# Another chunking of the score rows, and two block products that change places in the MoEs' up stages

## The chip, the cores and the metric

One core of a Trainium2 chip. The metric is the device time of one execution in microseconds, the median over runs.

## The reference

Attention with mixing over the heads, then two feed-forward stages ("MoEs" without routing), all in float32:

```python
scores = scale * np.matmul(q, k.transpose(0, 1, 3, 2))        # 4 x 12 x 448 x 448, head_dim 64
scores = np.einsum('bhij,hg->bgij', scores, w_pre)
scores = scores - np.max(scores, axis=-1, keepdims=True)
attn = np.exp(scores)
attn = attn / (np.sum(attn, axis=-1, keepdims=True) + 1e-09)
attn = np.einsum('bhij,hg->bgij', attn, w_post)
x = np.matmul(attn, v)                                        # then 1792 tokens x 768
...
h = x @ w_in                                                  # 768 -> 2048
y = (h * np.clip(h + 3.0, 0.0, 6.0) / 6.0) @ w_out            # 2048 -> 768
...
out = (((y @ w1) * (y @ w2)) @ w3) @ w_out2                   # 768 -> 1024 -> 1024 -> 768
```

## The kernel before, in words

**A planner writes the order.** Each piece of work is handed to `Plan.add` with its engine (or a choice of engines), a cost, a due time and its dependencies. `Plan.run` then plays the engines forward, takes on each the ready piece that is due first, and so writes out five fixed lists, one per queue: PE (TensorE), ACT (ScalarE), DVE (VectorE), POOL (GpSimd) and SP (the DMAs). On the chip every engine works its own list strictly in order and waits on semaphores. The table `URGE` (line 79) holds some 90 numbers that shift the due times; with other numbers all five lists come out differently, though the work is the same.

**Attention.** The query rows of a batch are cut into groups of ten rows; `GROUPS` (line 34) says how many groups each of four chunks has. `scores` (line 497) multiplies one chunk with the keys of two heads at a time, and ACT or DVE copies the result (sc) to the tile s. `mix` (line 531) works on a **slot** of two groups: SP gathers the rows of all heads of a group from s into g; PE mixes the heads (pre); DVE takes the row maximum; ACT the exponential, with its sum; DVE makes the weights wt from the sum; PE mixes and transposes again (post), and ACT or DVE copies that to pth or ptl. `values` (line 622) multiplies with v when half a batch (a unit) is done: three groups of four heads, each in two halves. Its result (val) is copied to one of two buffers x and stored to xdram by SP. Scores, pre, post, val and the later products share four PSUM buffers of two banks.

**MoEs.** A float32 product is three products of rounded parts (high x high, high x low, low x high). Two batches at a time go through a scheme of seven block products for eight, `seven` (line 892): with two PSUM tiles, `pair` (36 matmuls, 9 to a product) and `other` (27), it issues p1, p5, p6, p2, p3, p7 and p4. p1, p6, p7 and p4 go to the same bank of `pair`, p7 and p4 on top of what is there. ACT copies p1, p5 and p6 away (line 911: k1, k5, k6), since the next products add to those banks; DVE adds p2, p3 and p7 to the copies (line 914: c11 and c12 into t, c22 into v). p7 waits for k6, and p4 waits for c22. With `final` set, as the last output stage alone had it, p7 and c22 come before p3 and c12:

```python
k6 = keep(3, t, 1, cs, (p6,))
p2 = times(3, 4, as_, True, after=(p5,))
c11 = plus(4, t, 0, as_, (p2, k1))
p7 = times(5, 5 if final else 6, cs, False, after=(k6,))
c22 = plus(5 if final else 6, v, 0, cs, (p7, k5))
p3 = times(4, 6 if final else 5, bs, False, after=(k5, p7) if final else (k5,))
c12 = plus(6 if final else 5, t, 1, bs, (p3, k6))
p4 = times(6, 9, cs, False, after=(c22,))
```

`up_pair` (line 1007) is the first MoE's up stage for batches 1 and 2 (eight runs of `seven`; batches 0 and 3 go through a plain product beside it). `step` (line 1307) is the second MoE's up stage (sixteen runs); each next run's p1 may start after p7. Weights come as 64-bit floats and are turned to 32 bits by ACT and DVE (lines 790 to 802) all through the first MoE. Near the end of `step`, ACT and DVE also split and combine the inputs of the output stage (tiles orig, gh, act of 1792 elements).

Of the kernel before, what the change touches and what calls it, by code (L numbers as in the profile page):

```python
# [25 lines left out]
KC = DM // 128  # L26
# [4 lines left out]
ROWS = 12 * SET  # L31
GROUP = 2 * SET
BEFORE = 64 - ROWS
GROUPS = [12, 12, 11, 10]
G0 = [sum(GROUPS[:c]) for c in range(5)]
BLOCKS = (G0[4] + 1) // 2
LEN = [GROUP * g for g in GROUPS[:3]]
# [38 lines left out]
    return np.concatenate([order[u, :UNITS[u]] for u in range(2)])  # L76


URGE = dict(pPool=164.025, pACT=19693.834, pDVE=67507.971, pOut=433.371, pGuard=127.43, pCopy=293.188, pRest=69.604, pEvac=133.63, load0=-532.161, load=1034.863, gather=-351.175, pre=-489.029, max=-802.835, exp=-111.088, norm=-1250.143, post=102.75, evac=54.755, values=484.451, step=60.485, vload=1145.281, vload0=-1112.753, lead=-45.053, begin=89.262, consts=-98.616, moe=992.206, rows=1666.907, win=-476.319, wout=252.873, w34=-78.816, w2=109.341, unit0=29.551, unit1=70.923, down1=1322.478, unit2=1085.737, down2=538.008, wo=-207.504, wd=12.243, narrow=887.826, sums=1153.357, w34us=361.925, pHalf=138.291, halve=522.107, gsum=1604.135, joined=-2053.191, pairs=-159.136, lag=-1931.661, mix=-30.819, wo1=1020.065, stay=81.809, apart=2024.643, hHost=-16.855, hSP=788.66, hPE=152.667, hACT=95.962, hDVE=66.109, hPool=210.181, gatherA=-479.669, preA=428.762, maxA=391.052, expA=-367.699, normA=131.345, postA=215.656, evacA=537.477, gatherZ=1037.083, preZ=660.309, maxZ=151.309, expZ=3.296, normZ=1160.431, postZ=410.099, evacZ=-506.584, valuesA=-143.638, valuesZ=61.436, rowsZ=35.402, winZ=172.502, upZ=-145.507)


GS = ("g0", "g1", "g2", "g3")
# [184 lines left out]
def attention_moe(ctx: ExitStack, tc, qd, kd, vd, consts, w_in, w_out, w1, w2, w3t, w4, out):  # L267
# [409 lines left out]
    for ci in range(16):  # L677
        s0 = cstart[ci - 1] * U0 + URGE["begin"] if ci else -120
        s1 = cstart[ci] * U0 + URGE["lead"] if ci else -35
        for hp in range(H // 2):  # L680
            prio = s0 + hp * (s1 - s0) / 6
# [210 lines left out]
    def seven(prio, K, ws, xs, before, after=(), final=False):  # L892

        pair, other = Buf("up"), Buf("up")
        t, v = Buf("t"), Buf("v")
        cs, bs, as_ = (View(pair, lambda t: t[:, 0, :S]), View(other, lambda t: t[:, 0, :S]), View(other, lambda t: t[:, 1, :S]))

        def times(n, at, o, start, new=(), after=()):
            (bufs, parts), (xh, xl) = ws[n], xs[n]

            def emit():
                take(*new)
                for c in range(K):
                    wh, wl = (part()[:, col(c)] for part in parts)
                    mm(o(), wh, xh.t[:, c], start and c == 0, False, skip_group_check=not start)
                    mm(o(), wh, xl.t[:, c], False, False, skip_group_check=not start)
                    mm(o(), wl, xh.t[:, c], False, c == K - 1, skip_group_check=not start)
            return plan.add("PE", 600 * K, prio(at), emit, read=(*bufs, xh, xl), new=new, hold=(o.of,), after=after)

        def keep(at, x, k, o, after):  # L910
            return plan.add("ACT", 530, prio(at), lambda: nc.scalar.copy(x.t[:, k], o()), after=after, hold=(o.of, x))  # L911

        def plus(at, x, k, o, after):
            return plan.add("DVE", 620, prio(at), lambda: nc.vector.tensor_tensor(out=x.t[:, k], in0=o(), in1=x.t[:, k], op=ALU.add), after=after, hold=(o.of, x))  # L914

        p1 = times(0, 0, cs, True, (pair, t, v), (*before, *after))
        k1 = keep(0, t, 0, cs, (p1,))
        p5 = times(1, 1, bs, True, (other,), (p1,))
        k5 = keep(1, v, 0, bs, (p5,))
        p6 = times(2, 3, cs, False, after=(k1,))  # L920
# [8 lines that stand above are left out]
        return t, v, cs, p7, p4, (p2, p3), c11, c12, c22, keep  # L929
# [12 lines left out]
    rows, w_ins, w_outs, lasts = {}, {}, {}, {}  # L942
# [64 lines left out]
    def up_pair(fg, before):  # L1007

        at = M1 + F * fg + 2 * U1 + URGE["lag"]
        prio = lambda n: at + n * 2 * U1 / 7  # L1010
        t, v, cs, p7, p4, (p2, p3), c11, c12, c22, _ = seven(prio, KC // 2, joined1[fg], made1, before)
        r = Buf("rl")

        def relu(k, x, port, after):
            def emit():
                if k == 0:
                    take(r)
                nc.scalar.activation(out=r.t[:, k], in_=x(), func=ACTF.Relu, bias=3.0)
            return plan.add("ACT", 535, prio(6.5 + k * 2.5), emit, after=after, new=() if k else (r,), hold=(r, x.of), port=port)

        def gated(k, x, o, after, port):
            return plan.add("DVE", 620, prio(6.5 + k * 2.5), lambda: nc.vector.scalar_tensor_tensor(out=o(), in0=r.t[:, k], scalar=6.0, in1=x(), op0=ALU.min, op1=ALU.mult), after=after, hold=(r, x.of, o.of), port=port)

        def half(x, k):
            return View(x, lambda t: t[:, k])
        r2 = Buf("rl")

        def relu2():
            take(r2)
            nc.scalar.activation(out=r2.t, in_=t.t, func=ACTF.Relu, bias=3.0)  # L1030

        def gated2():
            nc.vector.scalar_tensor_tensor(out=t.t, in0=r2.t, scalar=6.0, in1=t.t, op0=ALU.min, op1=ALU.mult)
        a2 = plan.add("ACT", 918, prio(6), relu2, after=(c11, c12), new=(r2,), hold=(t,), port=True)
        g2 = plan.add("DVE", 1084, prio(6), gated2, after=(a2,), hold=(t, r2), port=True)
        a0 = relu(0, half(v, 0), True, (c22,))
        g0 = gated(0, half(v, 0), half(v, 0), (a0,), True)
        a1 = relu(1, cs, False, (p4, a0))
        g1 = gated(1, cs, half(v, 1), (a1,), False)
        b0, b1 = ORDER[2:]  # L1040
        gates[fg, b0] = gates[fg, b1] = [
            plan.add("SP", 1300, prio(7), lambda: nc.sync.dma_start(out=g1dram[fg, :, 1:3, 0], in_=t.t), after=(g2,), hold=(t,)),
            plan.add("SP", 700, prio(9), lambda: nc.sync.dma_start(out=g1dram[fg, :, b1, 1], in_=v.t[:, 0]), after=(g0,), hold=(v,)),
            plan.add("SP", 700, prio(9), lambda: nc.sync.dma_start(out=g1dram[fg, :, b0, 1], in_=v.t[:, 1]), after=(g1,), hold=(v,))]
        return (p7,), (p2, p3, p4)
# [248 lines left out]
    def blocks(prio, i):  # L1294

        same = lambda t: t
        wa, jb, wd, ja = (fetch(prio, "raw", (x, same), x.shape[-1], (after,)) for x, after in (
            (w2dram[i], kept["w2", i]), (jbdram[i], joined[i, 1]), (w1dram[i, :, 384:], kept["w1", i]), (jadram[i], joined[i, 0])))
        made = []
        for x, h in ((wa, 0), (jb, 0), (jb, 1), (wa, 1), (ja, 1), (ja, 0), (wd, 0)):  # L1300
            o = Buf("block")
            made.append(split(prio, 384, x, lambda x=x, h=h: f(x.t)[:, h * 384:(h + 1) * 384], (o,), lambda o=o: o.t[:, 0], lambda o=o: o.t[:, 1]))
        return made
# [3 lines left out]
    def step(pr, i, before, xs):  # L1307

        at = M2 + U2 * (8 * pr + i)
        prio = lambda n: at + n * U2 / 7  # L1310
        t, v, cs, p7, p4, p3, c11, c12, c22, _ = seven(prio, KC // 2, blocks(at + URGE["w2"], i), xs, before)

        def gate2(at, x, k, o, y, after, port):
            def emit():
                nc.vector.scalar_tensor_tensor(out=x.t[:, k], in0=o(), scalar=1.0 / 36.0, in1=y(), op0=ALU.mult, op1=ALU.mult)
            return plan.add("DVE", 620, prio(at), emit, after=after, hold=(o.of, y.of, x), port=port)

        g1 = gate2(9, t, 0, cs, View(t, lambda t: t[:, 0]), (p4, c11), False)
        g2 = gate2(6.5, t, 1, View(t, lambda t: t[:, 1]), View(v, lambda t: t[:, 0]), (c12, c22), True)
        pair_ = ORDER[2 * pr:2 * pr + 2]  # L1320
        for k, b in enumerate(pair_):
            gates2[i, b] = plan.add("SP", 700, prio(10), lambda k=k, b=b: nc.sync.dma_start(out=g2dram[i // 2, :, b, i % 2], in_=t.t[:, k]), after=((g1, g2)[k],), hold=(t,))
        return (p7,), p4
# [119 lines left out]
```

## Time and profile before

| what | before |
|---|---|
| median of 3 runs | 1187.79 us (1187.32 to 1189.89) |
| the profiled execution: time | 1183.64 us |
| the profiled execution: span, first to last instruction | 1181.8 us |
| mean granted TensorE clock | 0.994 of full |
| PE (TensorE) busy | 1148.5 us, 97% |
| DVE (VectorE) busy | 775.4 us, 66% |
| ACT (ScalarE) busy | 656.8 us, 56% |
| POOL (GpSimd) busy | 130.3 us, 11% |

The stages on PE: attention to about 361 us, the first MoE's up stage to 572, its down stage to 802, a product of two weight matrices to 869, the second MoE's up stage to 1077, the output to the end. Matmuls are pipelined and their ends are modelled, so that rows of one engine can overlap by some tenths of a microsecond; the idle time in brackets is the engine's own. "A <- B" after a wait names what ended it.

### The profile page before, as it was taken

Reading aid. Unit: us, or ns where it says so; the run is one execution under the profiler, and the core shown is the slowest. Engines: PE = TensorE matmul, PEld = TensorE weight load, DVE = VectorE, ACT = ScalarE, POOL = GpSimd, SP = SyncE. Lnnn points to the kernel's source line nnn. Section 1 sums busy time; section 2 is a strip of 40 time slices with the busy share of each in tenths; the row PEclk is TensorE's granted clock in tenths of the full one; section 3 lists DMA queues with packets and bytes.
Section 4 is the critical chain, followed back from the end, with each engine's and each line's share of the span. In section 5 each row is a group of like instructions: output and inputs, shape, how many; then the busy total and the mean of one; then the engine's idle time right before and its main releaser. Section 6 shows DMA issues by size and latency. Waiting matters only on the chain.

```text
span 1181.8 us, 28260 instructions
## 1 busy us (share of the span) xinstructions
PE 1148.5 (97%) x11376; PEld 978.2 (83%) x11376; DVE 775.4 (66%) x1290; ACT 656.8 (56%) x1262; POOL 130.3 (11%) x335
## 2 busy tenths in 40 slices
PE   8899989999899999999999999999999999999998
PEld 3476656666568999999999999998899998998998
DVE  3766555666478888848755557656754578479682
ACT  7778687787576666527545444434343344335452
POOL 1163343622111000001000000000000000000000
PEclk9999989999999999999999999999999999999999
DMA  6746655846665576747988889987965437478641
GB/s 221 221 148 232 173 191 175 250 169 195 200 205 181 166 255 205 244 152 240 330 286 316 263 312 342 323 291 244 315 218 158 130 129 277 143 234 276 211 153 70
DMA packets 132939, 261.36 MB, mean 221 GB/s; under 512 B 11880, under 2 KB 75208, under 8 KB 132808
## 3 DMA queue, kind: packets, MB, share of 16 engines
q1 hardware_dynamic: 132808, 259.55, 66.2%
q8 instruction: 89, 1.46, 0.5%
q14 instruction: 42, 0.34, 0.1%
HBM read 153.54 MB, written 67.26 MB: 187 GB/s over the span
## 4 chain that ended last, share of the span: by engine, by line
PE 88%; DMA 5%; DVE 3%; ACT 1%; issue 1%; SPq 1%; POOL 0%; DVEq 0%; ACTq 0%; POOLq 0%
PE up L275 41%; PE dn L275 19%; PE pre L275 6%; PE post L275 6%; PE sc L275 6%; PE w L275 5%; PE val L275 5%; DMA xdram<-x 1%; DMA stg<-xdram 1%; DMA raw<-w2dram 1%; DMA g<-s 1%; DMA both<-xdram 1%; DMA first<-w_in 1%; DVE act L278 0%; DVE t L914 0%
## 5 line engine op out<-in xcount | busy, mean ns | idle before, releaser
L275 PE MATMUL up<-act,block 128*128 128x448 f32 x1008 | 203.9, 364 | 4.8 <-DVE v L914 4.8
L275 PEld LDWEIGHTS up<-act,block 128*128 128x128 f32 x1008 | 190.2, 189 | 18.2 <-DVE v L914 5.5
L275 PE MATMUL dn<-gs,act 128*128 128x448 f32 x720 | 147.9, 362 | 0.0
L275 PEld LDWEIGHTS dn<-gs,act 128*128 128x128 f32 x720 | 135.1, 188 | 8.9
L275 PEld LDWEIGHTS post<-wt,e 60*64 60x64 f32 x5040 | 97.1, 135 | 52.9 <-issue 20.1
L275 PE MATMUL up<-act,wide 128*128 128x448 f32 x660 | 139.6, 364 | 0.6 <-DVE v L914 0.3
L275 PEld LDWEIGHTS up<-act,wide 128*128 128x128 f32 x660 | 123.1, 188 | 11.6 <-DVE v L914 1.1
L567 DVE TENSOR_REDUCE m<-pre 128x2 f32<-128x896 f32 (+1 forms) x92 | 99.8, 1088 | 44.5 <-PE pre L275 43.7
L573 ACT ACTIVATE e<-pre,m 128x448 f32<-128x448 f32 (+1 forms) x184 | 117.0, 641 | 11.0 <-DVE m L567 7.4
L412 ACT CAST block<-raw 128x384 fp32r<-128x384 f32 x107 | 54.6, 514 | 109.2 <-PE up L275 86.2
L275 PE MATMUL post<-wt,e 60*64 60x60 f32 x5040 | 100.7, 222 | 12.2 <-issue 6.9
L275 PE MATMUL pre<-g,wih 64*64 64x448 f32 x720 | 96.2, 568 | 6.2 <-ACT x L412 4.3
L790 ACT ACTIVATE raw<-raw 128x384 f32<-128x384 f32 (+1 forms) x140 | 70.6, 522 | 38.2 <-DMA raw<-w 23.9
L275 PE MATMUL up<-act,wb 128*128 128x448 f32 x432 | 87.6, 363 | 0.0
L275 PEld LDWEIGHTS up<-act,wb 128*128 128x128 f32 x432 | 81.0, 188 | 5.6 <-ACT t L911 0.3
L278 DVE TENSOR_TENSOR block<-raw,block 128x384 fp32r<-128x384 f32 x112 | 60.9, 554 | 34.8 <-ACT block L412 34.5
L914 DVE TENSOR_TENSOR t<-up,t 128x448 f32<-128x448 f32 x60 | 37.2, 621 | 66.2 <-PE up L275 61.2
L798 ACT ACTIVATE raw<-raw 128x768 f32<-128x768 f32 (+1 forms) x70 | 55.5, 795 | 41.8 <-DVE raw L796 41.7
L412 ACT COPY s<-sc 120x896 f32<-120x896 f32 (+2 forms) x77 | 68.3, 911 | 10.1 <-PE sc L275 9.6
L802 DVE SCALAR_TENSOR_TENSOR raw<-raw 128x384 int32<-128x384 int32 (+1 forms) x140 | 70.6, 538 | 1.4
L275 PE MATMUL dn<-gs,wo 128*128 128x448 f32 x336 | 71.1, 362 | 0.0
L275 PE MATMUL w<-wm,w 128*128 128x512 f32 (+1 forms) x384 | 66.6, 335 | 0.1
(137 smaller groups left out, 1713.7 us busy)
## 6 DMA issues: line engine op xcount, KB each, us to landing
g<-s SPq DMA_DIRECT2D x180, 210.0 KB
raw<-w SPq DMA_DIRECT2D x48, 384.0 KB
graw<-g1dram SPq DMA_DIRECT2D x32, 448.0 KB
raw<-w_out SPq DMA_DIRECT2D x32, 384.0 KB
raw<-w_in SPq DMA_DIRECT2D x28, 384.0 KB
g1dram<-t SPq DMA_DIRECT2D x24, 448.0 KB
raw<-w3t SPq DMA_DIRECT2D x32, 256.0 KB
vv<-vd SPq DMA_DIRECT2D x12, 640.0 KB
```

What stands on the lines that cost most here:

```text
L275: nc.tensor.matmul(o, lhsT=lt, rhs=rh, start=start, stop=stop, **kw)
L278: eng.tensor_tensor(out=o, in0=a, in1=b, op=ALU.subtract)
L412: nc.scalar.copy(o, i)
L567: nc.vector.tensor_reduce(out=m.t[used], in_=pre.t[used, :, :S], axis=AX.X, op=ALU.max, negate=True)
L573: nc.scalar.activation(out=e.t[used, a_], in_=pre.t[used, a_, :S], func=ACTF.Exp, bias=m.t[used, a_:a_ + 1], accum_out=z.t[used, a_:a_ + 1])
L790: nc.scalar.mul(value()[:, halves[i]], f(bits(i))[:, :, 1], 2.0 ** -112)
L798: nc.scalar.activation(out=f(y), in_=f(y), func=ACTF.Prelu, alpha=-2.0 ** 32)
L802: two(out=m.t[:, halves[i]], in0=bits(i)[:, :, 0], scalar=29, in1=m.t[:, halves[i]], op0=ALU.logical_shift_right, op1=ALU.bitwise_or)
L914: return plan.add("DVE", 620, prio(at), lambda: nc.vector.tensor_tensor(out=x.t[:, k], in0=o(), in1=x.t[:, k], op=ALU.add), after=after, h ...
```

## The change

The last two chunks of score rows get 12 and 9 groups for 11 and 10, `up_pair` and `step` call `seven` with `final=True`, and every number of `URGE` is another.

```diff
-GROUPS = [12, 12, 11, 10]
+GROUPS = [12, 12, 12, 9]
...
-URGE = dict(pPool=164.025, pACT=19693.834, pDVE=67507.971, pOut=433.371, pGuard=127.43, pCopy=293.188,
+URGE = dict(pPool=267.274, pACT=19707.749, pDVE=67519.092, pOut=411.463, pGuard=243.897, pCopy=232.932,
...
-        t, v, cs, p7, p4, (p2, p3), c11, c12, c22, _ = seven(prio, KC // 2, joined1[fg], made1, before)
+        t, v, cs, p7, p4, (p2, p3), c11, c12, c22, _ = seven(prio, KC // 2, joined1[fg], made1, before, final=True)
...
-        t, v, cs, p7, p4, p3, c11, c12, c22, _ = seven(prio, KC // 2, blocks(at + URGE["w2"], i), xs, before)
+        t, v, cs, p7, p4, p3, c11, c12, c22, _ = seven(prio, KC // 2, blocks(at + URGE["w2"], i), xs, before, final=True)
```

**The tenth of the sixteen runs in the second MoE, on PE.** up_11877 is this run's `pair`, up_11900 its `other`, up_11763 the `pair` of the run before and up_12017 that of the next. Before: p1, p5, the last run's p4, p6, p2, p3, p7, p4, and the next run's p1:

```order
L275 MATMUL up_11877<-act3_6285,block_11747 128x448 x9
L275 MATMUL up_11900<-act0_5554,block_11761 128x448 x9
L275 MATMUL up_11763<-act_6453,block_11723 128x448 x9
L275 MATMUL up_11877<-act0_5554,block_11775 128x448 x9
L275 MATMUL up_11900<-act_6453,block_11789 128x448 x9
L275 MATMUL up_11900<-act_6453,block_11802 128x448 x9
L275 MATMUL up_11877<-act_6453,block_11817 128x448 x9
L275 MATMUL up_11877<-act_6453,block_11835 128x448 x9
L275 MATMUL up_12017<-act3_6285,block_11846 128x448 x9
```

Now (`pair` up_11881, `other` up_11897):

```order
L275 MATMUL up_11881<-act3_6285,block_11750 128x448 x9
L275 MATMUL up_11897<-act0_5555,block_11765 128x448 x9
L275 MATMUL up_11769<-act_6453,block_11729 128x448 x9
L275 MATMUL up_11881<-act0_5555,block_11781 128x448 x9
L275 MATMUL up_11897<-act_6453,block_11799 128x448 x9
L275 MATMUL up_11881<-act_6453,block_11830 128x448 x9
L275 MATMUL up_11897<-act_6453,block_11813 128x448 x9
L275 MATMUL up_11881<-act_6453,block_11844 128x448 x9
L275 MATMUL up_12023<-act3_6285,block_11851 128x448 x9
```

p7 and p3 have changed places, so that p3 now stands between p7 and p4, and p2 alone between p6 and p7. The sixteenth run reads alike in both. In the other fourteen, 18 matmuls stood between p7 and p4 and 27 do now. In the first MoE these were 45, 9, 18, 18, 18, 18, 9 and 18, and are seven times 9 and once 27. Between p6 and p7 stood 18 in all but the very first run of seven; now 9.

**The same run on DVE.** t_11878 and v_11879 (now t_11882 and v_11883) are its t and v. Before:

```order
L914 TENSOR_TENSOR t_11878<-up_11900,t_11878 128x448
L278 TENSOR_TENSOR block_11979<-raw_11730,block_11979 128x384
L278 TENSOR_TENSOR orig_11853<-orig_11891,orig_11853 128x1792
L914 TENSOR_TENSOR t_11878<-up_11900,t_11878 128x448
L278 TENSOR_TENSOR block_11995<-raw_11742,block_11995 128x384
L914 TENSOR_TENSOR v_11879<-up_11877,v_11879 128x448
```

Now:

```order
L414 CAST gh_11971<-orig_11913 128x1792
L278 TENSOR_TENSOR block_11968<-raw_11673,block_11968 128x384
L278 TENSOR_TENSOR gh_11972<-orig_11913,gh_11971 128x1792
L914 TENSOR_TENSOR t_11882<-up_11897,t_11882 128x448
L914 TENSOR_TENSOR v_11883<-up_11881,v_11883 128x448
L278 TENSOR_TENSOR block_11984<-raw_11736,block_11984 128x384
L278 TENSOR_TENSOR block_11998<-raw_11748,block_11998 128x384
L914 TENSOR_TENSOR t_11882<-up_11897,t_11882 128x448
```

c22 stood sixth here, behind c11, a subtraction over 1792 elements, c12 and two blocks; now it follows c11 at once, and the large cast and subtraction that stand ahead of c11 are others. In the sixteenth run a cast over 1792 elements stands between c11 and c22, as it stood ahead of c22 before.

**ACT, where the third batch's value products begin** (ptl and pth are post's destinations by turns). Before:

```order
L573 ACTIVATE e,z<-pre,m 128x448 x2
L412 COPY x<-val 128x2x208 x2
L412 COPY s<-sc 120x896
L412 COPY ptl<-post 128x84x5
L412 COPY s<-sc 120x896
```

Now:

```order
L573 ACTIVATE e,z<-pre,m 128x448 x4
L412 COPY x<-val 128x2x208 x2
L412 COPY ptl<-post 128x84x5
L412 COPY x<-val 128x480
L412 COPY ptl<-post 128x84x5
L573 ACTIVATE e,z<-pre,m 128x448 x2
```

A third copy x has come close behind the first two. ACT has the same six rows one batch earlier, where before had a third copy x in that place too; PE and SP repeat there as well.

## Rows read from the trace of the kernel before

**Rows 1.** The page: span, PE's busy time, the second MoE's products (busy, mean ns, idle).

```profile
span 1181.8 us, 28260 instructions
...
PE 1148.5 (97%) x11376; PEld 978.2 (83%) x11376; DVE 775.4 (66%) x1290; ACT 656.8 (56%) x1262; POOL 130.3 (11%) x335
...
L275 PE MATMUL up<-act,block 128*128 128x448 f32 x1008 | 203.9, 364 | 4.8 <-DVE v L914 4.8
```

**Rows 2.** Busy time by stretch: PE, PEld, DVE, ACT, POOL, then clock, DMA share, GB/s.

```profile
130.00:160.00 30.00, 26.16 (x489) 17.59 (x492) 11.70 (x23) 14.98 (x36) 15.67 (x40) 0.89 0.80 241
...
361.00:572.00 211.00, 210.39 (x1052) 196.07 (x1049) 170.08 (x286) 128.87 (x217) 13.70 (x9) 1.00 0.65 215
...
869.00:1077.00 208.00, 203.24 (x1007) 189.78 (x1006) 133.49 (x222) 89.69 (x169) 0.00 (x0) 0.99 0.59 192
```

**Rows 3.** Who PE waited for: us in total, times, longest us.

```profile
PE post L275 <- issue: 6.9, 5, 2.3
...
PE pre L275 <- ACT x L412: 4.3, 2, 3.8
PE post L275 <- ACT s L412: 2.4, 1, 2.4
```

**Rows 4.** Timeline near 995 us, DVE and PE: start, us, engine, idle before.

```profile
992.21 2.02 DVE L278 TENSOR_TENSOR orig<-orig 128x1792 f32<-128x1792 f32 x1
...
995.14 0.62 DVE L914 TENSOR_TENSOR v<-up,v 128x448 f32<-128x448 f32 x1
...
995.82 4.47 PE L275 MATMUL up<-act,block 128*128 128x448 f32 x13 [2.85 <-DVE v L914]
```

**Rows 5.** Timeline near 1075 us.

```profile
1073.20 1.08 DVE L414 CAST act<-orig 128x1792 fp32r<-128x1792 f32 x1
...
1075.21 2.08 PE L275 MATMUL up<-act,block 128*128 128x448 f32 x9 [1.92 <-DVE v L914]
```

**Rows 6.** Busy time in two stretches of low clock, columns as in rows 2.

```profile
149.66:156.47 6.81, 4.76 (x74) 3.00 (x78) 2.42 (x5) 4.26 (x11) 3.64 (x8) 0.50 0.96 314
...
996.16:999.56 3.40, 3.40 (x11) 3.00 (x10) 2.78 (x4) 0.25 (x1) 0.00 (x0) 0.50 0.77 290
```

**Rows 7.** Timeline in the first MoE's up stage, near 409 and 501 us.

```profile
408.45 0.61 DVE L914 TENSOR_TENSOR v<-up,v 128x448 f32<-128x448 f32 x1
...
409.12 1.07 PE L275 MATMUL up<-act,wide 128*128 128x448 f32 x4 [0.17 <-DVE v L914]
...
501.37 1.88 PE L275 MATMUL up<-act,wide 128*128 128x448 f32 x8 [0.18 <-DVE v L914]
```

**Rows 8.** Timeline of ACT near 919 us, and of PE from 914.8 us.

```profile
919.20 0.51 ACT L412 CAST block<-raw 128x384 fp32r<-128x384 f32 x1 [1.28 <-PE up L275]
919.62 0.53 ACT L911 COPY t<-up 128x448 f32<-128x448 f32 x1
...
914.80 15.56 PE L275 MATMUL up<-act,block 128*128 128x448 f32 x77
```

**Rows 9.** Timeline of ACT near 300 us.

```profile
299.75 0.54 ACT L790 ACTIVATE first<-first 128x384 f32<-128x384 f32 x1 [2.75 <-DMA first<-w_in]
```

**Rows 10.** PE, SP, ACT from 143 to 152 us; without an engine: the chain of waits.

```profile
143.25 1.84 PE L275 MATMUL val<-pth,vv 128*64 128x240 f32 x20
...
147.00 0.87 PE L275 MATMUL sc<-khl,qhl 64*120 64x448 f32 x6
151.71 1.77 PE L275 MATMUL pre<-g,wih 64*64 64x448 f32 x8 [3.84 <-ACT x L412]
...
143.26 1.30 SPq L425 DMA_DIRECT2D vv<-vd  x1
...
144.68 6.32 DMA xdram<-x
...
151.10 0.56 ACT L412 COPY x<-val 128x480 f32<-128x480 f32 x1 [7.08 <-DMA xdram<-x]
```

**Rows 11.** Timeline of PE near 217 us.

```profile
216.81 1.40 PE L275 MATMUL pre<-g,wih 64*64 64x448 f32 x6 [0.45 <-DMA g<-s]
```

More of the change, by code (lines that the diff above doesn't have):

```diff
@@ L76, in token_order @@
     return np.concatenate([order[u, :UNITS[u]] for u in range(2)])
-URGE = dict(pPool=164.025, pACT=19693.834, pDVE=67507.971, pOut=433.371, pGuard=127.43, pCopy=293.188, pRest=69.604, pEvac=133.63, load0=-532.161, load=1034.863, gather=-351.175, pre=-489.029, max=-802.835, exp=-111.088, norm=-1250.143, post=102.75, evac=54.755, values=484.451, step=60.485, vload=1145.281, vload0=-1112.753, lead=-45.053, begin=89.262, consts=-98.616, moe=992.206, rows=1666.907, win=-476.319, wout=252.873, w34=-78.816, w2=109.341, unit0=29.551, unit1=70.923, down1=1322.478, unit2=1085.737, down2=538.008, wo=-207.504, wd=12.243, narrow=887.826, sums=1153.357, w34us=361.925, pHalf=138.291, halve=522.107, gsum=1604.135, joined=-2053.191, pairs=-159.136, lag=-1931.661, mix=-30.819, wo1=1020.065, stay=81.809, apart=2024.643, hHost=-16.855, hSP=788.66, hPE=152.667, hACT=95.962, hDVE=66.109, hPool=210.181, gatherA=-479.669, preA=428.762, maxA=391.052, expA=-367.699, normA=131.345, postA=215.656, evacA=537.477, gatherZ=1037.083, preZ=660.309, maxZ=151.309, expZ=3.296, normZ=1160.431, postZ=410.099, evacZ=-506.584, valuesA=-143.638, valuesZ=61.436, rowsZ=35.402, winZ=172.502, upZ=-145.507)
+URGE = dict(pPool=267.274, pACT=19707.749, pDVE=67519.092, pOut=411.463, pGuard=243.897, pCopy=232.932, pRest=10936.038, pEvac=162.974, load0=-965.088, load=917.044, gather=73.79, pre=-573.489, max=-937.682, exp=-237.144, norm=-1687.724, post=140.53, evac=882.498, values=532.272, step=155.526, vload=1973.472, vload0=-795.918, lead=-109.035, begin=95.349, consts=188.64, moe=1174.983, rows=2115.979, win=-554.95, wout=321.468, w34=32.664, w2=-1006.448, unit0=38.916, unit1=191.728, down1=1630.349, unit2=987.078, down2=671.427, wo=-224.433, wd=395.148, narrow=913.642, sums=644.111, w34us=597.076, pHalf=911.565, halve=381.083, gsum=911.99, joined=-2042.419, pairs=-340.427, lag=-2412.168, mix=-144.477, wo1=1492.112, stay=83.006, apart=2063.61, hHost=-2.784, hSP=819.446, hPE=161.58, hACT=96.688, hDVE=108.223, hPool=196.256, gatherA=-235.646, preA=559.106, maxA=82.868, expA=-355.798, normA=721.411, postA=-50.519, evacA=468.864, gatherZ=1801.716, preZ=717.905, maxZ=-315.441, expZ=-417.391, normZ=1753.918, postZ=396.417, evacZ=-422.963, valuesA=-206.805, valuesZ=1.489, rowsZ=-147.439, winZ=-12.543, upZ=-138.594)
 GS = ("g0", "g1", "g2", "g3")
```

## The prediction

> **What bounds the kernel now.** I read the page's first two parts, then the stretches, then who TensorE (PE) waits for, and then the timeline around each long wait. The page says it at once: PE is busy 1148.5 of 1181.8 us [rows 1], so 33 us of idling plus what a lowered clock costs is all that a change of order can win. The stretches say where that idling is [rows 2]. In the attention part, 130 to 160 us has 3.84 us without PE work and a mean granted clock of 0.89. In the first MoE's up stage, 361 to 572 us, PE misses 0.6 us of 211 and the clock is 1.00. In the second MoE's up stage, 869 to 1077 us, it misses 4.8 us. The causes: 4.8 us before the second MoE's products on VectorE's sums of line 914 [rows 1]; 6.9 us on "issue" (PE itself, no other engine), 4.3 us on ScalarE's copies x and 2.4 us on its copies s [rows 3]. The profiled execution took 1183.64 us (span 1181.8); the runs shown have a median of 1187.79 us, 4.15 us more. I sum against 1183.64 and carry the difference over.
>
> No work is added or dropped: the same matmuls, weight loads and DMAs are issued, in another order and with 120 and 90 query rows in the last two chunks for 110 and 100; a few casts and copies change between ScalarE, VectorE and GpSimd. So each term below is a wait that goes, stays or comes.
>
> **Term 1, the second MoE's up stage: p7 ahead of p3.** The fourth product p4 adds to the PSUM bank that the sum c22 (line 914, into v) reads after p7. In two of the sixteen steps of before, p4 stands right behind p7, with nothing between. There the trace shows the two long waits: 2.85 us at 995.82 [rows 4] and 1.92 us at 1075.21 [rows 5]. In the first, VectorE was in a 2.02 us subtraction when p7 ended, and c12 and a block still stood ahead of c22; in the second a 1.08 us cast did. Now p3, nine matmuls, stands between p7 and p4. Nine matmuls take 1.8 us (203.9 / 1008 x 9, [rows 1]), and VectorE has c22 ahead of c12. In the first step the 2.02 us subtraction now comes after c12, and a subtraction of like size ahead of c11 ends before p7 does if it starts where VectorE reached that place before. I take both waits as gone: 2.85 + 1.92 = 4.77 us. Bounds: if p3's 1.8 us only shorten them, 1.8 + 1.8 = 3.6 us; more than 4.77 is not there.
>
> [...] **Term 1: -6.5 us**, bounds -3.6 and -6.5.
>
> **Term 2, the same swap in the first MoE.** Seven of its eight runs of seven products now stand in one piece or nearly so, so c22 is covered by nine matmuls there; two runs of before had this, and both show a wait, of 0.17 us (at 409.12, 0.18 at 501.37 [rows 7]). In both c12 stood ahead of c22 on VectorE, and now it doesn't. So the cost is between nothing and 5 x 0.17 = 0.85 us; **+0.4 us**.
>
> **Term 3, the price of the swap: p7 now follows p6 sooner.** p7 overwrites what ScalarE must first copy away after p6 (line 911). That copy had p2 and p3 as its cover, 18 matmuls, and has p2 alone, 9, in 23 of the 24 runs. What a copy needs is on the rows: it starts 0.42 us after the cast that the end of a product releases, and ends 0.53 us later, 0.95 us in all (919.20 to 920.15) [rows 8]; PE runs on meanwhile, 77 matmuls without a wait. The cover of 1.8 us leaves 0.85 us. **0**; upper bound, if every one of the 23 waited as c22 did with the same cover, 23 x 0.17 = +3.9 us. Cover gone would be two more casts in front.
>
> **Term 4, the end of attention.** At 299.75 ScalarE stood 2.75 us behind a DMA (the first weights) with two copies s queued behind it, and PE waited 2.4 us for those [rows 3, 9]. The new ScalarE order puts that scaling two and a half slots later, behind the copies s, and its load on SP two slots later; what PE does then is a run of four halves of value products. Late next would be a copy x, with those products as cover. **-2.4 us**, bounds 0 and -2.4.
>
> **Term 5, the middle of attention.** At 151.71 PE waited 3.84 us [rows 10]. The row's chain: three copies x in close order, but x has two buffers; the first store to xdram stood on SP behind a load of v, issued at 143.26, and itself went out at 144.68 and took 6.32 us to land; the third copy waited on ScalarE until 151.10, and all that stood behind it, so that no PSUM buffer came free. The clock then was 0.50 from 149.66 to 156.47, with 4.76 us of PE work, 2.4 us lost [rows 6]. 3.84 + 2.4 = 6.2 us. The new order keeps this place as it is, in batch 2, and, as the ScalarE rows show, **writes the same pattern into batch 3**, where before two copies x and then copies s and ptl stood; SP's list repeats too (load of v, store, load of v, store). There the stretch lost 0.45 us on a gather [rows 11], which the moved chunk border takes away. A product of values now stands where scores stood ahead of the waiting product, 1.84 for 0.87 us [rows 10]: 1.0 us more cover. So 6.2 - 0.45 - 1.0 = **+4.8 us**, bounds 0 (the store lands in time) and +6.2.
>
> **Term 6, the rest.** The border of the last chunk moves one slot later; the first gather of a batch keeps at least two runs of 18 score matmuls and two of post as cover. The "issue" waits are 6.9 us [rows 3], most of them where PE's order is unchanged row by row; **0**, bounds of a quarter of them, 1.7 us, either way.
>
> **The sum:** -6.5 + 0.4 + 0 - 2.4 + 4.8 = -3.7 us, 1183.64 to 1179.9 us; on the runs' level 1187.79 - 3.7 = **1184.1 us**. A measurement of this kernel tells 0.2% (2.4 us) from no change, so faster means under 1185.4 and slower over 1190.2.
>
> **The rivals.**
> *A, the late store doesn't repeat in batch 3.* For it: only one of three batches shows it, and the DMA share was 0.80 in that stretch [rows 2]. Against it: the order repeats row by row. Then -8.5 us, 1179.3 us. Chance 0.20.
>
> *B, slower: the copy after p6 comes late.* Place: ScalarE ahead of p7, 23 times. Price: term 3's copy needs 0.95 of 1.8 us; with two more casts in front, 1.0 us, PE waits some 0.2 us, and in the first MoE, where ScalarE was busy 129 of 211 us [rows 2], with a third cast (0.51 us, [rows 8]) as well, some 0.7 us: 16 x 0.2 + 7 x 0.7 = 8.1 us. It decides from 0.27 us each on (6.1 / 23). For it: that busy share. Against it: the copies after p1 had the same cover in five runs and PE shows no wait for them. -3.7 + 8.1 = 1192.2 us; chance 0.16.
>
> *C, VectorE is late for c22 all the same.* In both steps of term 1 a 1.08 us cast and, in one, a 2.02 us subtraction stand shortly ahead of it. If each runs a microsecond or two later, a wait of 1 us is left at both places and the clock falls as before: 2 + 1.7 us given back, about 1187.8 us, no change. Chance 0.12.
>
> *D, a new wait in attention of the size of term 5 elsewhere*, for instance where value products now hold a PSUM buffer among the slots: +6.2 us, 1190.3 us. Chance 0.08.
>
> *E, the clock swings in the MoEs.* Waits of 0.17 and 0.18 us in the first MoE left the granted clock at 1.00 over 211 us [rows 2, 7]. If short waits at the 23 places lowered it each time as the 2.85 us wait did [rows 6], that is 23 x 1.7 = 39 us, 1223 us. Chance 0.02.
> [...]
>
> **How the numbers follow.** The forecast has 0.42. The likeliest time is its own, 1184.1. The range is 1178 to 1191: up, it takes in term 3's bound, C and D, and leaves out the upper part of B; down, it takes in A to its middle and beyond, and leaves out A with the two later issue waits gone too; with E that is under 0.2. Faster: three quarters of the forecast (its terms spread some 2 us around -3.7, against a threshold of -2.4) and A, 0.52. No change: most of C, the rest of the forecast, the milder part of D, 0.24. Slower: B, half of D, E and the bad end of terms 3 and 5, 0.24.
>
> **What would show it.** Right: no wait over 0.3 us before p4 in the second MoE and a clock of 1.00 from 869 to 1077 us; no wait of 2.4 us on copies s near 300 us; two waits of 3 to 4 us for x, one near 150 and one some 85 us later, each with a clock of 0.50 behind it. Wrong: PE waits on copies of line 911 (B), on line 914 still (C), or the second wait for x missing (A).

## The result, and the profile after

The changed kernel takes 1167.7 us (median of 6 runs, 1165.87 to 1175.97) beside 1187.55 us for the kernel before: a ratio of 0.9852, 95% interval 0.9826 to 0.9878. That is 17.6 us faster by the ratio and 19.9 by the medians. The forecast was 3.7 us faster, in a range that ended 10 us above the result. The profiled execution took 1170.31 us.

The page of the changed kernel, to be held against [rows 1]:

```profile
span 1168.5 us, 28243 instructions
...
PE 1143.3 (98%) x11376; PEld 976.0 (84%) x11376; DVE 777.7 (67%) x1296; ACT 658.2 (56%) x1263; POOL 116.8 (10%) x328
...
L275 PE MATMUL up<-act,block 128*128 128x448 f32 x1008 | 202.1, 362 | 1.2 <-DVE v L914 1.2
```

The wait on line 914 fell from 4.8 to 1.2 us, where term 1 had it at nothing. PE's busy time fell too, by 5.2 us, for the same 11376 matmuls. Some 3 us of that is the lowered clock (half of PE's busy time at a granted clock of 0.50: 5.8 us before, 2.8 now); the rest says that something else had made PE slow while it counted as busy. The list of whom PE waited for (us, times, longest), against [rows 3]:

```profile
PE post L275 <- issue: 6.7, 6, 1.8
...
PE post L275 <- ACT e L573: 3.4, 1, 3.4
PE up L275 <- DVE v L914: 1.2, 1, 1.2
PE val L275 <- DMA vv<-vd: 1.0, 1, 1.0
```

No wait on a copy x and none on ScalarE's copies s is left; a wait on an exponential has come. The stretches, columns as in [rows 2]:

```profile
130.00:160.00 30.00, 28.21 (x630) 20.11 (x630) 14.07 (x25) 17.41 (x45) 20.43 (x53) 1.00 0.75 229
...
860.70:1063.80 203.10, 201.85 (x1010) 188.88 (x1009) 136.89 (x220) 88.80 (x169) 0.00 (x0) 1.00 0.61 197
```

Between 130 and 160 us PE ran 630 matmuls where it had run 489, at full clock. The border was expected to stall PE twice on a copy x, and does so neither time; 1.78 us on "issue" stand at the first one, 1.03 us on a load of v at the second (226.54), and neither is there in a second profile. The first border's third copy x (PE's timeline, and ACT's beside it):

```profile
146.35 0.46 PE L275 MATMUL post<-wt,e 60*64 60x60 f32 x11 [1.78 <-issue]
...
147.00 0.56 ACT L412 COPY x<-val 128x480 f32<-128x480 f32 x1 [5.16 <-DMA xdram<-x]
```

ScalarE still waits 5.16 us for the store of x, where it waited 7.08 [rows 10], and the copy starts 4.1 us earlier; PE shows no wait for it.

**Where the time went.** I counted PE's work by the matmul (pre at 100.3 ns, post 17.3, values 74 or 89, scores 132.5, MoE products 200.5) and read off when each kernel reached the same amount. The table gives, by stretch of the kernel before, how much sooner (-) or later (+) than in its first profile, in us; the sums agree with the spans. "After again" and "before again" are second profiles of the two kernels.

```
stretch of before            after  after  before  spacing  2nd MoE
                                    again  again   only     only
0-64 us                       -0.5   -0.9   -1.1    +0.1     -3.5
64-123                        +0.7   +0.7   +0.9    +0.9     +2.2
123-172, border to batch 3    -6.2   -8.3   +0.7    -7.3      0.0
172-297, border to batch 4    -2.9   -4.0   -1.5    -0.8     -2.0
297-377, end of attention     +0.7   -1.7   +0.6    -3.0     +2.4
377-887, first MoE to w3 w4   +0.3   -0.5   +0.4    +0.4     +0.5
887-end, second MoE, output   -5.4   -5.4   +1.6    +2.9     -5.9
sum                          -13.3  -20.1   +1.6    -6.9     -6.4
```

Two parts carry it: the borders (third and fourth rows), where I had forecast no change and a loss of 4.8 us, and the second MoE. The columns to the right are experiments, below.

### The profile page after: what moved, and what is told of

It reads as the page before. It is cut to its first block, busy times and chain, and to the rows that moved or that the text cites. A ratio compares the mean times of both kernels' runs of the same rounds, so it can differ in the third digit from the quotient of the medians.

```text
span 1168.5 us, 28243 instructions
## 1 busy us (share of the span) xinstructions
PE 1143.3 (98%) x11376; PEld 976.0 (84%) x11376; DVE 777.7 (67%) x1296; ACT 658.2 (56%) x1263; POOL 116.8 (10%) x328
## 4 chain that ended last, share of the span: by engine, by line
PE 94%; DMA 2%; DVE 2%; issue 1%; ACT 1%; SPq 0%; ACTq 0%
PE up L275 43%; PE dn L275 20%; PE post L275 7%; PE sc L275 6%; PE pre L275 6%; PE w L275 6%; PE val L275 6%; DMA stg<-xdram 1%; DMA vv<-vd 1%; DVE act L278 0%; DMA k<-kd 0%; ACT ptl L412 0%; DVE t L1067 0%; SPq L552 0%; DVE s L414 0%
## 5 line engine op out<-in xcount | busy, mean ns | idle before, releaser
L275 PEld LDWEIGHTS dn<-gs,act 128*128 128x128 f32 x696 | 130.5, 187 | 8.7
L275 PE MATMUL pre<-g,wih 64*64 64x448 f32 x720 | 90.3, 558 | 0.8 <-DVE ptl L414 0.8
L412 ACT COPY s<-sc 120x896 f32<-120x896 f32 (+1 forms) x75 | 66.2, 912 | 9.5 <-PE sc L275 9.2
L275 PEld LDWEIGHTS dn<-gs,wo 128*128 128x128 f32 x336 | 63.0, 188 | 4.2
```

The lines of the kernel that those rows point to most:

```text
L275: nc.tensor.matmul(o, lhsT=lt, rhs=rh, start=start, stop=stop, **kw)
L412: nc.scalar.copy(o, i)
```

## What the trace had shown, and I had not read

At 119.6 us both kernels have done the same work, within 0.2 us. The stretch from there to 133.5 us, before:

```profile
119.60:133.50 13.90, 13.90 (x332) 8.82 (x322) 11.13 (x19) 11.58 (x30) 1.06 (x5) 1.00 0.50 135
```

and after:

```profile
119.60:133.50 13.90, 13.90 (x364) 8.98 (x356) 12.21 (x21) 12.49 (x32) 1.07 (x5) 1.00 0.64 223
```

PE is busy throughout in both, at full clock, and does 332 matmuls in one and 364 in the other. PE's timeline of before shows how that can be:

```profile
127.45 1.36 PE L275 MATMUL pre<-g,wih 64*64 64x448 f32 x6
128.25 0.43 PE L275 MATMUL post<-wt,e 60*64 60x60 f32 x8
128.65 0.54 PE L275 MATMUL pre<-g,wih 64*64 64x448 f32 x2
...
132.94 1.51 PE L275 MATMUL pre<-g,wih 64*64 64x448 f32 x6
```

Eight matmuls pre take 0.98 us where nothing holds them; here six take 1.36 and 1.51 us. They read g, which the gathers fill, and the gathers are late in small steps that never make a gap: the two for the eight matmuls that begin at 127.45 landed at 127.11 and 128.18, and the last two of the eight ran at 128.65. DMA is no busier for it: 135 GB/s against 223. The trace's landing records of one gather, the first of the third chunk in batch 2 (us from issue; ten, as many as it has rows; one more, at 1.19 us in all four, is left out):

```
before, rows 11 apart        2.60 2.65 2.66 2.68 3.22 3.24 3.59 3.65 3.70 4.02
before again, 11 apart       2.61 2.66 2.67 2.68 3.23 3.24 3.60 3.67 3.71 4.03
after, 12 apart              2.61 2.63 2.65 2.66 2.67 2.68 2.69 2.70 2.71 2.72
before, spacing 12           2.61 2.63 2.65 2.66 2.67 2.68 2.69 2.70 2.71 2.72
```

A gather takes ten rows out of s, as far apart as the chunk has groups (line 546: `d = GROUPS[c]`). Its packets are the same in every chunk (1792 bytes), yet in the records from 119.7 to 126 us of before 196 of 411 took 70 to 75 ns and 176 took 120 to 150 ns; after, 625 of 655 took 70 to 75 ns and none over 120. Over batches 2 to 4 of before the fastest gather landed in 2.7 us with rows 12 apart, and in 4.0 and 4.1 us with 11 and 10; after, in its four chunks in 2.8, 3.9 (2.8 in a second profile), 2.7 and, 9 apart, 2.7 us. SP, which issues them one by one, was held too: one issue took a median of 1.17 us before and 0.77 us after (119.4 to 130 us). So the chunk sizes set more than how much work a chunk holds: they set from which partitions a gather reads.

The third chunk's last gather in batch 4 of before, issued 5.3 us behind the one before it, shows the same: two rows landed by 2.65 us, the others between 3.38 and 4.17 us; after, the same gather, the eleventh of that chunk, had all ten between 2.68 and 2.80 us. The gathers 10 apart overlap with others, and single rows tell nothing there. Why rows 11 apart land later is not in the trace.

## The experiments

**Does the loss belong to the program or to one execution?** The kernel before, unchanged.

> The kernel before, unchanged, profiled a second time. Question: which of its waits belong to the program and which to one execution. Theory G (the gathers): the gathers of the third and fourth chunk of a batch, whose rows lie 11 and 10 partitions apart in s, took a median of 5.4 to 7.4 us from issue to landing in the first profile, against 2.7 us at best for rows 12 apart, and PE lost 2.2 us near 130 us and 2.2 us near 217 us behind them; both come back here, and so do the store wait of some 3.8 us near 150 us and the two waits on line 914 in the second MoE (2.8 and 1.9 us). Rival L (luck): the wait near 150 us hangs on one late store and is gone or below 1 us in this execution, and the fastest gathers of the third and fourth chunk land in 2.7 us like the others.

The profiled span was 1183.5 us. The gathers of the third and fourth chunk landed in 3.95 and 4.00 us at best, and the wait for x came back (3.29 us, at 151.97), as did 2.85 and 1.91 us on line 914. In the stretch from 119.6 us:

```profile
119.60:133.50 13.90, 13.81 (x318) 8.55 (x310) 10.91 (x19) 11.66 (x29) 1.06 (x5) 1.00 0.51 138
```

The loss belongs to the program; luck (rival L) is out. The wait of 0.45 us on a gather near 217 us [rows 11] did not come back as a gap, while PE did the work of 205 to 225 us only 0.8 us faster than in the first profile, of the 2.2 us that it had been put at: the gap was the visible part.

**The spacing alone.**

```diff
-WIDE = [GROUP * d for d in GROUPS]
+STEP = [12, 12, 12, 12]; WIDE = [GROUP * d for d in STEP]
...
-                    order[WD0[c] + t + GROUPS[c] * r] = row
+                    order[WD0[c] + t + STEP[c] * r] = row
...
-            size = S // 2 if isinstance(n, tuple) else n.stop - n.start
+            size = S // 2 if isinstance(n, tuple) else GROUP * GROUPS[b % 4]
...
-            p0, d = G - G0[c], GROUPS[c]
+            p0, d = G - G0[c], STEP[c]
```

(The third edit only keeps the planner's costs, and so every list, as they were.)

> The kernel before with one thing changed: the rows of a group lie 12 partitions apart in s in every chunk (for 11 and 10 in the third and fourth), with unused columns between them; the order on every engine is that of before, row by row. Theory G: gathers of the third and fourth chunk land in 2.7 to 3 us at best for 4.0, the 2.2 us near 130 us and the 2.2 us near 217 us go, and with SP and the gathers earlier at least half of the store wait near 150 us with its low clock (6.2 us) goes: 6 to 10 us faster than before. Rival O (the order of the fitted table does it, the spacing nothing): within 1.5 us of before. Rival W (wider chunks cost): slower by up to 1 us, from larger loads of q.

1172.52 us beside 1184.27: ratio 0.9891 (0.9864 to 0.9918). Without the new table, the new chunk sizes or the exchange, some 12 of the 18 to 20 us are there, more than the 6 to 10 that theory G gave. The stretch, and PE's timeline in it:

```profile
119.60:133.50 13.90, 13.90 (x366) 9.17 (x360) 11.75 (x23) 12.88 (x32) 1.06 (x5) 1.00 0.59 214
```

```profile
128.19 0.98 PE L275 MATMUL pre<-g,wih 64*64 64x448 f32 x8
...
130.76 0.98 PE L275 MATMUL pre<-g,wih 64*64 64x448 f32 x8
...
146.15 0.46 PE L275 MATMUL post<-wt,e 60*64 60x60 f32 x12 [0.92 <-issue]
```

Eight pre in 0.98 us again, and no wait for x near 150 us, with every list in the order of before. Theory G holds in its direction, O and W fall. Of its two places near 130 and 217 us, the first gave back 2.3 us in this profile, the second 0.9 of the 2.2 us expected. The profiled execution gained only 6.9 us, in part since its clock fell to 0.50 behind both waits in the second MoE (2.9 us more lost there, table).

**Which chunk?** The same edit with `STEP = [12, 12, 12, 10]`:

> The kernel before with rows 12 apart in the third chunk only (11 groups); the fourth keeps its spacing of 10, the order stays. If the third chunk's gathers carry the gain (they stand right ahead of a batch's border, where SP then has the next loads and the stores of x behind them): 6 to 12 us faster than before, no wait for x above 2 us near 150. If each chunk carries its share: some 6 us. If the fourth carries it: within 2 us of before.

and with `STEP = [12, 12, 11, 12]`:

> The kernel before with rows 12 apart in the fourth chunk only (10 groups); the third keeps its spacing of 11. Complement of the run with the third alone: the two gains together should come to the 12.9 us of both. If the third chunk carries it, this one is within 3 us of before and keeps a wait for x above 3 us near 150.

The third alone: 1172.79 us beside 1185.97, 0.9887 (0.9859 to 0.9916), all of it. The fourth alone: 1183.71 us, 0.9981 (0.9958 to 1.0004), not told from nothing; its profile keeps a wait for x:

```profile
154.03 1.77 PE L275 MATMUL pre<-g,wih 64*64 64x448 f32 x8 [5.26 <-ACT x L412]
```

The third chunk carries it. That its place decides (its gathers stand right ahead of the border, with SP and PE close behind them) is a reading: the two chunks also differ in spacing, 11 and 10, and no run exchanges the two.

**Was the store's place on SP the cause, as term 5 had it?** In this run, otherwise the kernel before, the store goes out ahead of three gathers and the load of v. (A second edit, not shown, marks that store as `first`.)

```diff
-        self.end = now
+        self.end = now; sp = [o for o in order if o["eng"] == "SP"]; at = next(i for i, o in enumerate(sp) if o.get("first")); late = sp[at - 4:at]; order = [o for o in order if o not in late]; at = order.index(sp[at]); order[at + 1:at + 1] = late
```

> The kernel before with SP's list changed in one place, at the border before 150 us: the store of x for which the third copy waits goes out ahead of the three last gathers and the load of v that stood before it. Theory of the prediction's term 5 (PE's wait of 3.3 to 4.2 us there hangs on that store's place on SP): the store goes out some 5 us earlier, the wait is gone or below 1 us with the low clock behind it, 3.5 to 6.5 us faster than before. Rival (the gathers themselves, late by their spacing, hold PE up there, and the store is only the last of what is late): less than 2 us, with a new wait on a gather, on v or on x in the same place.

1185.39 us beside 1185.97: 0.9997 (0.9974 to 1.0021), nothing. SP's, ACT's and PE's timeline:

```profile
139.51 1.65 SPq L667 DMA_DIRECT2D xdram<-x  x1
141.25 3.60 SPq L552 DMA_DIRECT2D g<-s  x3
...
149.19 1.80 SPq L552 DMA_DIRECT2D g<-s  x2
...
145.91 0.56 ACT L412 COPY x<-val 128x480 f32<-128x480 f32 x1 [1.51 <-DMA xdram<-x]
...
158.38 1.50 PE L275 MATMUL pre<-g,wih 64*64 64x448 f32 x8 [2.51 <-DMA g<-s]
```

The store went out at 139.51 for 144.68, the third copy x ran 5.2 us earlier and PE's wait for it was gone. The three gathers put back (issued from 141.25) landed by 149.43, in time. But the next pair went out at 149.19 and 150.11, where before had them at 147.86 and 148.78, and landed at 158.24 and 158.86: PE waited 2.51 us for these and 1.44 us on VectorE's copy ptl behind them, and the eight pre behind the first of these waits took 1.50 us for 0.98. In before they landed at 156.12 and 157.19, so a PE that came as early would have waited there too, if less long. The wait for x was a place where the lateness of SP's list came out, not its cause. The rival holds.

**The exchange.** In both MoEs, with the old table and chunks:

> The kernel before with only the exchange of p7 and p3 in both MoEs; attention keeps its order row by row. Theory: the second MoE's two waits on line 914 shrink or go with the low clock behind the first, 4.4 to 6.5 us, and the first MoE's two waits of 0.17 us do too: 4 to 6.5 us faster than before. Rival (the gain came from the fitted table, the exchange only moves the wait to p7 behind the copy of line 911): within 1.5 us of before, or slower by up to 4 us.

1181.9 us beside 1184.27: 0.997 (0.9953 to 0.9988), 3.6 us by the ratio and a little under what the theory gave. In the second MoE alone:

> The kernel before with the exchange of p7 and p3 in the second MoE alone; PE's and POOL's rows up to there are the same, and of DVE's and ACT's only those of that stage move. Theory (term 1): the waits of 2.8 and 1.9 us on line 914 go, with the low clock behind them (1.7 us or twice that): 4.8 to 8 us faster than before. Rival (copy of line 911 late for p7, sixteen times 0.2 us): 3 us less gain. Rival (the exchange gives only 3.6 us as in both MoEs together): 2 to 4 us.

1179.48 us beside 1186.85: 0.9942 (0.9921 to 0.9962), 6.9 us by the ratio, and in its profile:

```profile
868.00:1075.00 207.00, 206.94 (x1036) 193.68 (x1035) 140.97 (x225) 91.77 (x172) 0.00 (x0) 1.00 0.60 197
```

Both waits on line 914 and the low clock are gone there, 6.6 us at equal work (0.7 us come back in the output), and no copy of line 911 holds PE up. With the exchange in both, the second MoE's stage gains the same 6.6 us, but the first MoE's planned order changes throughout and the profile loses 2.7 us between 380 and 620 us of before (0.3 us at a copy of line 911), most in one wait:

```profile
584.08 3.28 PE L275 MATMUL dn<-gs,wo 128*128 128x448 f32 x15 [1.52 <-DVE gs L278]
```

With the new table the first MoE had 0.9 us less than before in both profiles; that the refit repaired there what the exchange moved is likely, not shown. The changed kernel without the exchange:

> The changed kernel with the exchange of p7 and p3 undone in both MoEs; attention keeps the changed kernel's order row by row. If the attention part of the change gave 8 us and the exchange 5: some 8 us faster than before in the profile's terms (12 us on the runs' level, where the whole is 17 to 20 us), 4 to 6 us slower than the changed kernel. Rival (nearly all comes from the exchange, directly or through the clock): within 2 us of before.

1177.47 us beside 1184.27: 0.9932 (0.9906 to 0.9957), 8.1 us faster by the ratio where the theory wanted some 12, and some 10 us slower than the changed kernel by the medians where it wanted 4 to 6. The rival falls, but the theory's two sizes were off. The profile says why: up to 361 us it is 10.2 us ahead of before, and loses 5.8 us of that again, 4.0 in the second MoE and the output. There the new table without the exchange waits 2.85 us and then longer than before had:

```profile
1068.61 3.07 PE L275 MATMUL up<-act,block 128*128 128x448 f32 x9 [3.51 <-DVE v L914]
```

So in the new table the exchange is worth more than in the old one.

**Spacing made bad again in the changed kernel.** First the changed kernel itself, as the level; then with the spacing edit and `STEP = [12, 12, 12, 11]`:

> The changed kernel once more, on the same chip as the three runs below, as their level: 1.2 to 1.7% (14 to 20 us) faster than before, with waits of 1.2 us on line 914 in the second MoE and of 3.4 us on an exponential near 318 us as in its first profile. If those two differ by more than 1 us, they belong to one execution.

> The changed kernel with the rows of its last chunk (9 groups) 11 partitions apart instead of 9, nothing else, the order row by row the same. [...] Rival S (12 and 9 are good only because the chunks have other sizes and so another order): gathers land as before, within 1.5 us of the changed kernel.

The changed kernel: 1166.91 us beside 1186.85, 0.9837 (0.981 to 0.9865). With the last chunk's rows 11 apart: 1169.92, 0.9861 (0.9831 to 0.9891). Its last chunk's gathers landed in 4.02 us at best for 3.03, and it is 3 us slower by the medians, but the intervals overlap: theory G, by which spacing alone would cost 2 to 7 us, has the direction, not shown apart from nothing.

**Do the two add up, and what is the table worth?** Before with spacing 12 and the exchange in the second MoE:

> Before with rows 12 apart everywhere and the exchange in the second MoE alone, with the old table and the old chunk sizes. If the two effects add up: 12.9 + 4.8 to 8 = 17.7 to 21 us faster than before, that is as fast as the changed kernel or up to 3 us faster, so that the refitted table gives nothing of its own. Rival (the refitted table itself gains some 4 us or more): the changed kernel stays ahead by 3 us or more.

1167.52 us beside 1186.85: 0.9845 (0.9817 to 0.9872), 18.4 us by the ratio, so the two effects add up (12.9 + 6.9) as near as the intervals tell. It is as fast as the changed kernel within what was measured, and does not beat it: no gain of the refitted table by itself is seen. Its profile has a wait for x of 2.06 us at 147.72: spacing does not always take that wait away whole. The old table with the new chunk sizes and the same exchange:

> The kernel before with the changed chunk sizes (12, 12, 12 and 9) and the exchange in the second MoE alone, with the old table: another order in attention than either kernel. Theory G: chunk sizes bring the gain through the gathers, whatever the order, so 15 to 21 us faster than before, like the changed kernel. Rival (the table has to be refitted to the new sizes): 8 us or less of gain, with a new wait in attention of 3 us or more.

1180.45 us beside 1185.97: 0.996 (0.9941 to 0.9979), less than the exchange alone gave. Its gathers landed well (2.7 and 2.8 us), and until 330 us of before it was 13 us ahead; then it lost 18 us at the end of attention, in part at this wait, with a granted clock of 0.50 from 343.92 to 354.16:

```profile
345.92 1.77 PE L275 MATMUL post<-wt,e 60*64 60x60 f32 x28 [4.49 <-DVE wt L589]
```

Theory G as I put it there ("whatever the order") falls. The new sizes make another order, which the old table ends badly; they need the refit. The spacing needs none.

## Why the prediction was wrong

- **Term 5 (+4.8 us) failed, in its sign.** It left the border in batch 2 as it was (the table's third row) and put 4.8 us on the one in batch 3 (the fourth). Measured were -6.2 and -2.9 us, -9.1 together; in the second profile -8.3 and -4.0, -12.3 together. Its reading was that the store's place on SP makes the wait and that a repeated order repeats it. The order did repeat; but the third chunk's gathers, with rows 12 apart, land 1.3 us sooner at best (in batch 2 2.6 us by their median, 2.87 for 5.44), PE does not slow down at 127 us, and SP reached the store at 138.10 us instead of 144.68. The price of 6.2 us was near (the spacing alone won 5.0 us from 140 to 172 us of before; waits of 3.3 to 5.3 us came in every profile with before's SP list and rows 11 apart in the third chunk), its cause was not.
- **The step ahead of all terms failed with it**: that no work is added or dropped, so that each term is a wait. A DMA with the same packets from other partitions was other work here (70 to 75 ns for most packets with rows 12 apart, 120 to 150 ns for 176 of 411 with rows 11 apart). I took the new row counts (120 and 90 for 110 and 100) for sizes and never asked what else `GROUPS` enters (line 546).
- **Term 1 (-6.5 us) was right but for one wait**: -5.4 us in both profiles of the changed kernel, -6.6 us alone. The difference is the wait in the tenth run, which shrank from 2.85 to 1.25 us and stayed:

```profile
980.75 2.02 DVE L278 TENSOR_TENSOR gh<-orig,gh 128x1792 fp32r<-128x1792 f32 x1
985.08 0.62 DVE L914 TENSOR_TENSOR t<-up,t 128x448 f32<-128x448 f32 x1 [2.32 <-PE up L275]
985.62 0.61 DVE L914 TENSOR_TENSOR v<-up,v 128x448 f32<-128x448 f32 x1
...
986.29 3.88 PE L275 MATMUL up<-act,block 128*128 128x448 f32 x18 [1.25 <-DVE v L914]
```

  The large subtraction ended in time, as the term said; c11 ahead of c22 then waited for PE until 985.08. That is 0.04 us after the end of the product right ahead of p4, which is p3; p2, the product that c11 adds, had ended at 981.44. Why c11 started only behind p3 is open. Rival C (VectorE late for c22) so came true at one of its two places, at 1.25 us and with the granted clock at 1.00 behind it (986.29 to 1020 us). No run shows by itself the 1.7 us that term 1 has beyond the two waits, and that rivals C and E use: it was my estimate, half of 3.40 us of PE work at a granted clock of 0.50 [rows 6]. In the trace 13 matmuls from 995.82 on took 4.47 us [rows 4], where 13 at 200.5 ns are 2.6 us.
- **Term 2 (+0.4 us)**: the first MoE's up stage measured -0.9 us. **Term 3 (0)** held: PE shows no wait on line 911 in the changed kernel. Rival B is out, and so is E: the clock stayed at 1.00 through the second MoE (323.8 to 1166 us).
- **Term 4 (-2.4 us)**: the wait on s went, but "late next" was not a copy x under cover. A cast act<-stg stood ahead of an exponential on ScalarE, waiting for its load (the chain of waits of the changed kernel):

```profile
311.76 5.32 DMA stg<-xdram
...
317.11 0.57 ACT act L412
317.67 0.64 ACT e L573 x2
...
318.35 1.65 PE post L275 x50
```

  PE waited 3.4 us (2.4 in the second profile), and in the first profile the granted clock was 0.50 from 317.1 to 323.8 us; the stretch measured +0.7 and -1.7 us. With the spacing alone, in the order of before, the wait on s was gone too and the stretch measured -3.0 us, so the new ScalarE order need not be what removed it.
- **Term 6 (0)** held in sum, +0.2 and -0.2 us up to 123 us.
- **Rival A**, that the wait does not repeat, had the right direction and 9 to 12 us too small a size (1179.3 us): it kept the first of the two waits.

Terms 1 to 4 and 6 together, -8.5 us, stand against -4.2 and -7.8 us measured; term 5 stands against -9.1 and -12.3. It is off by 14 to 17 us, more than the whole miss of the two profiles (9.6 and 16.4 us).

## What to carry to other kernels

When a table or a size changes, list every address that is computed from it before pricing waits; here a stride between partitions was worth more (12.9 us by the ratio) than the exchange in the order (6.9). A busy share of 100% does not tell the speed (332 and 364 matmuls in the same 13.9 us): count the matmuls in a stretch and divide, and where the same instruction takes longer than elsewhere, look at what feeds it. And where one wait has a queue ahead of it that is late, moving the last piece forward may only move the wait, as the store moved ahead of the gathers did (ratio 0.9997).

## What was not expected of the hardware

Gathers of the same bytes in the same packets landed at best in 2.7 us or in 4.0 us by the spacing of the partitions they read. In the stretch read (119.7 to 126 us) 625 of 655 packets took 70 to 75 ns with rows 12 apart; 11 apart, 176 of 411 took 120 to 150. The lowered clock behind a wait was no fixed price here: behind the same 1.91 us wait near 1075 us it fell to 0.50 with the spacing alone (2.9 us more from 887 us to the end) and fell in the second profile of before (1.6 us more), and stayed at 1.00 in the first (999.6 to 1180.4 us); with the spacing in the third chunk alone it fell neither there nor behind the 2.85 us wait (mean granted clock 0.999 over the span). Single profiles of one kernel lay 6.7 us apart (spans of 1168.5 and 1161.8 us of the changed one), so a single trace places a gain but does not size it.
